# First chunk's end in another order on ScalarE and VectorE, and the upper half of the second ssm_k asked for by ScalarE

## The chip, the core and the metric

One core of one Trainium2 chip runs the whole program in one launch. The metric is the device time of an execution in microseconds; the time before is the median of three runs. Five engines work side by side, each through its own instruction stream in order: TensorE (PE), VectorE (DVE), ScalarE (ACT), GpSimd (POOL) and SyncE (SP). SyncE issues nearly all transfers; ScalarE has a queue for transfers of its own.

## The reference

Sequence length S = 2048, width D = 640, all in float32. The first block is an H3 layer with a short and a long causal convolution, the second a token-mixing MLP; both sit behind a layer norm whose scale and shift come from a conditioning vector c.

```python
mod = (_silu(c) @ w_mod).reshape(c.shape[0], 6, 1, -1)      # sa, ca, ga, sb, cb, gb
h = _layernorm(x) * (1 + ca) + sa
# _A_ref(h, k, v, ...):
k_shift = sum(k_pad[:, t:t + S, :] * shift_k[:, ks - 1 - t] for t in range(4))
kv = k_shift * v
y = irfft(rfft(kv, 2 * S) * rfft(ssm_k, 2 * S))[:S] + kv * ssm_D     # along S, per channel
x = x + ga * (h * y)
h = _layernorm(x) * (1 + cb) + sb
x = x + gb * (gelu(h^T @ w1 + b1) @ w2 + b2)^T
```

## The kernel before

The 640 channels are cut into five chunks of 128 (`c` = 0 to 4). For each chunk the long convolution is a product of transforms, made by matmuls: `step1` is the first stage of the forward transform (side 0 for kv, side 1 for ssm_k, four groups `t` each), `f2` the second stage together with the product (eight groups `g`), `i2` and `i1` the two stages back. `gate` multiplies the result by A1, the normed and scaled input, and adds it to x. After the last chunk come the second layer norm and the MLP, which fill the rest of the time with matmuls.

The order of instructions on every engine is the order in which the Python code calls them. There is no scheduler: an engine that waits at one instruction holds back all that stands behind it in its stream. The names that matter here:

- `load_ks(c)` asks for the ssm_k of a chunk, in two halves of 64 channels and 512 KB (L151), each in rows of 32 elements, and then for the two rows of ssm_D (L154), 256 bytes each. All four stand on SyncE. The data go to `KSR`, the lower columns of the tile `aux`.
- `perm_add` adds ssm_D to the first element of each channel (two operations of one partition, on VectorE for c = 1), and `perm` (L163, ScalarE) reorders the whole ssm_k into `KSP`, the tile `p`, from which `step1(1, t)` reads.
- `taps` (L169, ScalarE) spreads the four taps of the short convolution; `load_taps` fetches the next ones.
- `ac` are 16 scalings of 128 columns of x into A1 on ScalarE (L289, the first eight from tile `xa`, the others from `xb`); `po` are four multiplies and adds on VectorE, two for each half of A1, with the rows G1 and G0 that `mod_row` has made (copies on ScalarE in L360 and L362, two products on VectorE).
- `fill` is a list of the short convolution's operations for the next chunks, of which `dv(n)` puts n on VectorE. `kv_ops(2, pool)` puts one of the four groups on GpSimd.
- PSUM has three slots in rotation (`ring`). The slot of a `step1` group can be that of an `i1` half, and is then free once `gate` has read it.

The first chunk (c = 0) is special: its A1, the sums of w_mod and the mod rows all stand at its end, together with the step1 of the second chunk's kv and ssm_k. ssm_k of the second chunk goes into columns of `aux` that w_mod held, so that it can be asked for only when `mod_part` of kk = 2 has read them.

Every transfer counts on one of eight semaphores, taken in turn. A request waits for the transfer that held its semaphore last, eight requests back in the program.

Of the kernel before, what the change touches and what calls it, by code (L numbers as in the profile page):

```python
# [49 lines left out]
def mixer_kernel(ctx: ExitStack, tc: tile.TileContext, q, k, v, shift_k, ssm_k, ssm_D, w1, b1, w2, b2, c,  # L50
# [7 lines left out]
    act, dve, pool, pe, sync = nc.scalar, nc.vector, nc.gpsimd, nc.tensor, nc.sync  # L58
# [31 lines left out]
    KSR = T_aux[:, 0:2048]  # L90
# [54 lines left out]
    def load_taps(c, eng=sync):  # L145
        for h in range(2):
            eng.dma_start(TR[64 * h:64 * h + 64], dram(shift_k, (DC * c + 64 * h) * 4, [[0, 64], [1, 256]]))

    def load_ks(c, eng=sync):
        for h in range(2):  # L150
            sync.dma_start(KSR[64 * h:64 * h + 64].rearrange("p (i n) -> p i n", i=64),  # L151
                           dram(ssm_k, (DC * c + 64 * h) * S, [[32, 64], [S, 64], [1, 32]]))
        for h in range(2):
            eng.dma_start(DR[64 * h:64 * h + 1], dram(ssm_D, DC * c + 64 * h, [[64, 1], [1, 64]]))  # L154


    def perm_add(c, eng=pool):
        for h in range(2):
            r = KSR[64 * h:64 * h + 1].rearrange("p (i n) -> p i n", i=64)[:, :, 0]
            TT(eng, r, r, DR[64 * h:64 * h + 1], ALU.add)  # L160
# [6 lines left out]
    def taps():  # L167

        act.activation(TAP, TR.rearrange("p (i s) -> p s i", s=4), AF.Copy)  # L169
# [84 lines left out]
    def i2(r, eng=None):  # L254

        pp = [psum(), psum()]
        for s in range(8):
            for ri in range(2):
                for qd in range(4):
                    p = slice(32 * qd, 32 * qd + 32)  # L260
                    o, i = 512 * (qd % 2) + 64 * s, 2 * (8 * r + s)
                    pe.matmul(pp[qd // 2][:, o:o + 64], Y[p, ri, i:i + 2].rearrange("p i k -> p (i k)"),  # L262
                              V2[p, 64 * ri:64 * ri + 64], start=ri == 0, stop=ri == 1)
        for qd in range(4):
            a = 16 * (qd // 2) + 8 * r
            o = T2[:, a:a + 8, :, qd % 2]
            i = pp[qd // 2][:, 512 * (qd % 2):512 * (qd % 2) + 512].rearrange("p (a m) -> p a m", a=8)
            if eng is not None and qd > 1:
                eng.tensor_scalar(o, i, 1.0, None, op0=ALU.mult)
            else:  # L270
                act.activation(o, i, AF.Copy)  # L271
# [189 lines left out]
    def run(ops):  # L461
        for f_ in ops:
            f_()
# [47 lines left out]
    for c in range(NC):  # L511
        cn = c + 1 if c + 1 < NC else None
        ac, po = a1_ops(c)
        pend_m = pend_a = None
        for g in range(8):
            m_, a_ = f2(g)
            if pend_m:
                pend_m()
            if pend_a:
                pend_a()  # L520
            pend_a, pend_m = (pend_m and pa_next), m_
            pa_next = a_
            if c:
                for f_ in ac[2 * g:2 * g + 2]:
                    f_()
            if cn is None and g < 4:

                act.activation(X[:, 512 * g:512 * g + 1], epsc, AF.Copy)
                for b in range(2):
                    sync.dma_start(X[64 * b:64 * b + 64, 512 * g:512 * g + 512],  # L530
                                   dram(w1, (16 * b + g) * F, [[32 * F, 64], [1, 512]]))
            dv(-(-len(fill) // max((6 if c else 8) - g, 1)))
            if c and cn is not None and g == 3:
                perm_add(cn)
        pend_m()
        if pend_a:
            pend_a()
        pa_next(dve if c else pool)
        if c == 0:
            for j in range(16):  # L540
                for h in range(2):
                    dve.bn_stats(bst[:, j, h, :], XR(j, 320 * h, 320))
                dve.bn_aggr(mv[:, j, :], bst[:, j, 0:2, :])
        if c and c + 2 < NC:
            taps()
            if c + 3 < NC:
                load_taps(c + 3)
        if c == 0:
            mod_load(0, 4, P[:, 0:1920])
            for t in range(4):  # L550
                step1(0, t)
            ps = psum()
            pe.transpose(ps[:, 0:36], stg, ID[0:36, 0:36])
            act.activation(cols, ps[:, 0:36], AF.Copy)
            act.activation(sil, cols[:, 30:35], AF.Silu)
            i2(0)
            for kk in range(4):
                mod_part(tap, kk, pl[kk])
                if kk == 1:
                    sync.dma_start(T_v1[:, 0:4096], c_v1, max_dma_last_dim=4096)  # L560
                if kk == 2:
                    load_ks(1)
            rstd(rs1, nm1, 0, 16)
            run(ac[0:4])
            i2(1)
            mod_part(tap, 4, pl[4])
            load_k(2, 1)
            load_k(2, 2)
            load_v(2, 2)
            load_halo(2)  # L570
            load_k(2, 0)
            load_v(2, 0)
            load_v(2, 1)
            load_k(2, 3)
            load_v(2, 3)
            mod_sum(tap, T_kt[:, 0:640])
            run(ac[4:8])
            pool.tensor_scalar(PW, TR.rearrange("p (i s) -> p s i", s=4), 1.0, None, op0=ALU.mult)
            run(kv_ops(2, pool))
            for i in range(3):  # L580
                mod_row(i, T_kt[:, 0:640])
            taps()
            load_taps(3)
            perm_add(1, dve)
            perm(1)
            load_ks(2)
            run(ac[8:16])
            run(po[0:2])
            fill.extend(kv(3, ((0,), (1, 2), (3,))))
        elif cn is not None:  # L590
            for t in range(2):
                step1(0, t)
            perm(cn)
            if c + 2 < NC:
                fill.extend(kv(c + 3 if c + 3 < NC else None))
            else:
                fill.extend(x1s(cc, j) for cc in range(c) for j in range(16))
        else:
            blk.update({f: (j16(t[:, 0:2048]), j16(t[:, 2048:4096])) for f, t in (
                (0, mem("w0", 4096, "wb0")), (1, mem("w1", 4096, "wb1")))})  # L600
            mod_load(3, 3, T_z[:, 0:1920])
            mod_load(3, 4, P[:, 0:1920])
            for kk in range(3):
                mod_part(tap, kk, pl[kk])
            t = mem("in", 4288, "wb3")
            blk[3] = j16(t[:, 0:2048]), j16(t[:, 2048:4096])
            split_rows(0, X, (0, 1, 3))
            split_rows(1, T_aux[:, 0:2048], (0, 1, 3))
            run(po)
        if c:  # L610
            dv(7 if cn is not None else 8)
            i2(0)
            if cn is None:
                mod_part(tap, 3, pl[3])
                i2(1, dve)
                t = mem("y", 4096, "wb2")
                blk[2] = j16(t[:, 0:2048]), j16(t[:, 2048:4096])
                split_rows(0, X, (2,))
                split_rows(1, T_aux[:, 0:2048], (2,))
                break  # L620
            run(po)
            step1(0, 2)
            i2(1)
            step1(0, 3)
            dv(3)
        if c and c + 2 < NC:
            load_ks(c + 2)
        if cn == NC - 1:
            pl = [piece(T_in, 3), piece(T_in[:, 1920:3840], 3), piece(T_t, 2) + [T_rows], three(T_z),
                  three(P)]  # L630
            for kk in range(2):
                mod_load(3, kk, (T_in[:, 0:1920], T_in[:, 1920:3840])[kk])
            for j in range(3):
                sync.dma_start(pl[2][j], dram(w_mod, 256 * 6 * D + 640 * (3 + j), [[6 * D, 128], [1, 640]]))
            load_rows(1, T_aux[:, 0:2048])
        for half in range(2):
            ps = i1(half)
            if c and half:
                dv(3)
            elif c:  # L640
                k0 = step1(1, 0, True)
            elif half:
                run(po[2:4])
            gate(c, ps, half)
        spill(c)
        if c:
            k0()
        for t in range(1 if c else 0, 4):
            step1(1, t)
        if cn == NC - 1:  # L650
            dv(12)
            fill.extend(x1s(c, j) for j in range(16))
        else:
            dv(11 if c else 8)
# [397 lines left out]
    for s in range(NW):  # L1052
        i = NF + s
# [84 lines left out]
```

## Time and profile before

| | |
|---|---|
| three runs, median | 700.57 us (697.78 to 703.14) |
| profiled execution | 697.86 us |
| its span, first to last instruction | 696.1 us |
| mean granted TensorE clock | 0.975 |
| busy: PE / DVE / ACT / POOL | 89% / 71% / 42% / 18% of the span |
| the five chunks | up to about 293 us |
| HBM traffic | 72.55 MB read, 10.49 MB written |

A row of a timeline gives start and length in us, engine, line, operation, output and input, the number of merged instructions and, in brackets, the idle time ahead of it with what ended it. An `SPq` or `ACTq` row is the time that an issue takes on SyncE or ScalarE, not the transfer's. A row that begins with two times joined by a colon sums a window: its length, then the busy time and number of instructions of PE, PE's weight loads, DVE, ACT and POOL, the granted clock, the share of the transfer engines and GB/s. A row of one line's instructions gives the least, median and longest duration in ns.

### The profile page before, as it was taken

The numbers are of one execution on the slowest core, as the hardware profiler recorded it, in microseconds if no ns is written. First come the engines' busy times: TensorE is split into PE (matmuls) and PEld (weight loads), VectorE is DVE, ScalarE is ACT, GpSimd is POOL, SyncE is SP. The second block draws the span as 40 slices with busy tenths as digits, with TensorE's granted clock in tenths as the row PEclk, the third lists the DMA queues.
The fourth block names the chain that finished last, engine by engine and source line by source line (L and its number), as shares of the span: only waits on it lengthen the run. The fifth ranks groups of instructions, "written<-read, shape, count | busy, mean of one in ns | idle before, by whom it ended". The sixth has DMA issues, their size and how long they took to land.

```text
span 696.1 us, 20691 instructions
## 1 busy us (share of the span) xinstructions
PE 622.0 (89%) x9099; PEld 595.8 (86%) x9099; DVE 496.1 (71%) x866; ACT 291.6 (42%) x464; POOL 128.2 (18%) x147
## 2 busy tenths in 40 slices
PE   0689777898998988888899999999999989999997
PEld 0688466788988888778899979999999989999997
DVE  6769448978979449888985741123499868888986
ACT  0444373554746536456666232232244233233331
POOL 5184018513425025000100000000000430000000
PEclk9999798999999999999999999999999999999999
DMA  9988988627443424171305604433353533466611
GB/s 183 243 227 232 381 169 178 145 43 155 91 79 111 145 64 121 59 153 32 60 1 91 121 2 99 84 61 64 110 141 104 167 121 99 121 173 172 167 44 38
DMA packets 166930, 84.37 MB, mean 121 GB/s; under 512 B 91030, under 2 KB 157368, under 8 KB 166840
## 3 DMA queue, kind: packets, MB, share of 16 engines
q1 hardware_dynamic: 162292, 81.74, 46.9%
q10 hardware_dynamic: 4548, 1.31, 1.1%
q8 instruction: 71, 1.16, 0.7%
q14 instruction: 19, 0.16, 0.1%
HBM read 72.55 MB, written 10.49 MB: 119 GB/s over the span
## 4 chain that ended last, share of the span: by engine, by line
PE 62%; DVE 17%; DMA 6%; ACT 5%; SPq 4%; issue 3%; POOL 1%; ACTq 0%; POOLq 0%; DVEq 0%
PE pst L436 20%; PE pst L997 17%; PE pst L1074 7%; PE pst L218 5%; PE pst L233 4%; PE pst L262 4%; SPq L496 3%; DVE tap L59 3%; PE pst L282 2%; DVE p L59 2%; DMA aux<-in_A_ssm_k_dram 2%; DVE kt L59 2%; DMA w<-in_const_w_dram 1%; DMA aux<-in_w_mod_dram 1%; DVE aux L59 1%
## 5 line engine op out<-in xcount | busy, mean ns | idle before, releaser
L233 PE MATMUL pst<-z,w 128*64 128x64 f32 x2560 | 79.0, 223 | 12.0 <-ACT z L220 5.7
L233 PEld LDWEIGHTS pst<-z,w 128*64 128x64 f32 x2560 | 76.8, 138 | 14.8 <-issue 7.7
L220 ACT ACTIVATE z<-pst 128x1024 f32<-128x1024 f32 x40 | 43.0, 1076 | 51.4 <-PE pst L218 51.3
L218 PE MATMUL pst<-v,x 128*64 128x128 f32 x640 | 39.6, 282 | 27.2 <-DVE x L59 24.1
L218 PEld LDWEIGHTS pst<-v,x 128*64 128x64 f32 x640 | 36.9, 142 | 28.1 <-POOL t L459 23.6
L59 DVE TENSOR_TENSOR p<-pst,kt 128x512 f32<-128x512 f32 x80 | 50.9, 680 | 12.7 <-ACT kt L237 9.3
L59 POOL TENSOR_TENSOR y<-p 128x256 f32<-128x256 f32 x72 | 51.1, 744 | 38.8 <-DVE p L59 38.6
L218 PE MATMUL pst<-v,p 128*64 128x128 f32 x640 | 39.7, 283 | 6.8 <-DVE aux L59 4.6
L997 PE MATMUL pst<-r_z,m_w 128*128 128x320 f32 x222 | 42.1, 312 | 2.2 <-DVE m_w L59 2.2
L218 PEld LDWEIGHTS pst<-v,p 128*64 128x64 f32 x640 | 37.2, 143 | 8.0 <-DVE aux L59 4.9
L262 PEld LDWEIGHTS pst<-v,y 32*128 32x128 f32 x1280 | 39.7, 194 | 3.8 <-issue 2.6
L237 ACT ACTIVATE kt<-pst 128x512 f32<-128x512 f32 x40 | 23.9, 599 | 43.7 <-PE pst L233 30.1
L262 PE MATMUL pst<-v,y 32*128 32x64 f32 x1280 | 41.6, 279 | 0.7 <-ACT z L220 0.6
L833 ACT ACTIVATE pst<-pst,sm 128x640 f32<-128x640 f32 x13 | 10.0, 767 | 75.8 <-PE pst L436 75.8
L985 ACT ACTIVATE m_w<-m_v 128x896 fp32r<-128x896 f32 x24 | 22.7, 951 | 37.0 <-PE pst L997 16.8
L997 PEld LDWEIGHTS pst<-r_z,m_w 128*128 128x128 f32 x222 | 35.2, 190 | 2.4 <-DVE m_w L59 2.4
L59 DVE TENSOR_TENSOR tap<-tap,kt 128x512 f32<-128x512 f32 x51 | 35.5, 696 | 1.3
L59 DVE TENSOR_TENSOR kt<-in,tap 128x512 f32<-128x512 f32 x51 | 34.9, 685 | 1.4
L59 POOL TENSOR_TENSOR m_p<-u_i,r_z 128x320 f32<-128x320 f32 x1 | 0.9, 882 | 183.4 <-issue 183.4
L271 ACT ACTIVATE z<-pst 128x512 f32<-128x512 f32 x38 | 20.9, 646 | 21.9 <-PE pst L262 21.9
L59 DVE TENSOR_TENSOR m_w<-m_v,m_w 128x896 fp32r<-128x896 f32 x24 | 27.9, 1164 | 2.4 <-ACT m_w L985 1.9
L436 PE MATMUL pst<-r_z,wb0b 128*128 128x320 f32 x180 | 28.2, 310 | 0.9 <-DVE u_x L59 0.9
(289 smaller groups left out, 1445.0 us busy)
## 6 DMA issues: line engine op xcount, KB each, us to landing
x<-in_B_w_dram SPq DMA_DIRECT2D x20, 512.0 KB
aux<-in_A_ssm_k_dram SPq DMA_DIRECT2D x10, 512.0 KB
in<-in_A_k_dram SPq DMA_DIRECT2D x36, 128.0 KB
in<-in_A_v_dram SPq DMA_DIRECT2D x36, 128.0 KB
m_x<-xs SPq DMA_DIRECT2D x28, 160.0 KB
out_dram<-m_x SPq DMA_DIRECT2D x28, 160.0 KB
w<-in_const_w_dram SPq DMA_DIRECT2D x2, 2048.0 KB
m_v<-in_B_w_dram SPq DMA_DIRECT2D x9, 448.0 KB
```

Of the source, the lines that this page charges most:

```text
L59: TT = lambda eng, o, a, b, op: eng.tensor_tensor(o, a, b, op=op)
L218: pe.matmul(ps[64 * ri:64 * ri + 64, o:o + 255:2], lhs, F1[:, 128 * ri:128 * ri + 128], start=True, stop=True)
L220: evac = lambda: act.activation(Z[:, side, t], ps.rearrange("p (a k e) -> p a k e", a=4, e=2), AF.Copy)
L233: pe.matmul(ps[64 * h:64 * h + 64, o:o + 64], W2[k1 // 32][:, 2 * (k1 % 32) + ri], rhs, start=True, stop=True)
L237: act.activation(kt.rearrange("p (m i) -> p m i", i=32), pv[:, :, 1], AF.Copy)
L262: pe.matmul(pp[qd // 2][:, o:o + 64], Y[p, ri, i:i + 2].rearrange("p i k -> p (i k)"), V2[p, 64 * ri:64 * ri + 64], start=ri == 0, stop=ri ...
L271: act.activation(o, i, AF.Copy)
L436: pe.matmul(ps[0:m, h, 0:320], w_.bitcast(F32R), r_[:, 320 * h:320 * h + 320].bitcast(F32R), start=first and i == 0, stop=last and i == 2)
L496: sync.dma_start(XH[j // 8][64 * b:64 * b + 64, j % 8], dram(q, (16 * b + j) * D, [[32 * D, 64], [1, D]]))
L985: act.activation(W[n][0].bitcast(F32R), A[p, w_], AF.Copy)
L997: pe.matmul(bank[n], w[:, i].bitcast(F32R), r.bitcast(F32R), start=i == 0 and k == 0, stop=i == 6 and k == 2)
L1074: pe.matmul(acc[s][:, h, 0:320], w[:, f_].bitcast(F32R), u[r + h].bitcast(F32R), start=f_ == 0 and k == 0, stop=f_ == NF - 1 and k == 2)
```

## The change

Two things change, both at the end of the first chunk. `load_ks` gets an argument `halves`: with the lower half alone it asks for that and for ssm_D on SyncE, with the upper half alone it asks for it on ScalarE. The second call stands behind the first four scalings. And the scalings, the first half of `po` and perm change places: three scalings ahead of the mod rows instead of four, the other nine directly behind them, ahead of taps and perm; the first two operations of `po` ahead of `perm_add`.

```diff
-    def load_ks(c, eng=sync):
-        for h in range(2):
-            sync.dma_start(KSR[64 * h:64 * h + 64].rearrange("p (i n) -> p i n", i=64),
+    def load_ks(c, eng=sync, halves=(0, 1)):
+        for h in halves:
+            (act if len(halves) == 1 and h else sync).dma_start(KSR[64 * h:64 * h + 64].rearrange("p (i n) -> p i n", i=64),
                            dram(ssm_k, (DC * c + 64 * h) * S, [[32, 64], [S, 64], [1, 32]]))
-        for h in range(2):
+        for h in range(2) if 0 in halves else ():
             eng.dma_start(DR[64 * h:64 * h + 1], dram(ssm_D, DC * c + 64 * h, [[64, 1], [1, 64]]))
...
                 if kk == 2:
-                    load_ks(1)
+                    load_ks(1, halves=(0,))
             rstd(rs1, nm1, 0, 16)
             run(ac[0:4])
+            load_ks(1, halves=(1,))
             i2(1)
             mod_part(tap, 4, pl[4])
...
             mod_sum(tap, T_kt[:, 0:640])
-            run(ac[4:8])
+            run(ac[4:7])
             pool.tensor_scalar(PW, TR.rearrange("p (i s) -> p s i", s=4), 1.0, None, op0=ALU.mult)
             run(kv_ops(2, pool))
             for i in range(3):
                 mod_row(i, T_kt[:, 0:640])
+            run(ac[7:16])
             taps()
             load_taps(3)
+            run(po[0:2])
             perm_add(1, dve)
             perm(1)
             load_ks(2)
-            run(ac[8:16])
-            run(po[0:2])
             fill.extend(kv(3, ((0,), (1, 2), (3,))))
```

ScalarE at the first chunk's end, before: the scalings (L289), the eviction of i2 (L271), mod_sum (L346), the mod rows, taps, perm (L163), the last eight scalings and the first step1 of ssm_k (L220).

```order
L289 ACTIVATE aux<-xa,sm 128x128 x4
L271 ACTIVATE z<-pst_931 128x512 x2
L271 ACTIVATE z<-pst_932 128x512 x2
L346 ACTIVATE kt<-tap 96x640
L289 ACTIVATE aux<-xa,sm 128x128 x4
L360 ACTIVATE g<-pst_1039 128x640
L362 ACTIVATE g<-pst_1043 128x640
L169 ACTIVATE tap<-rows 128x256
L163 ACTIVATE p<-aux 128x32x2x32
L289 ACTIVATE aux<-xb,sm 128x128 x8
```

And the same place with the change:

```order
L289 ACTIVATE aux<-xa,sm 128x128 x4
L151 DMA aux<-in_A_ssm_k_dram 64x64x32
L271 ACTIVATE z<-pst_931 128x512 x2
L271 ACTIVATE z<-pst_932 128x512 x2
L346 ACTIVATE kt<-tap 96x640
L289 ACTIVATE aux<-xa,sm 128x128 x3
L360 ACTIVATE g<-pst_1038 128x640
L362 ACTIVATE g<-pst_1042 128x640
L289 ACTIVATE aux<-xa,sm 128x128
L289 ACTIVATE aux<-xb,sm 128x128 x8
L169 ACTIVATE tap<-rows 128x256
L163 ACTIVATE p<-aux 128x32x2x32
```

The request of the upper half stands between the first scalings and the eviction of i2, and perm is the last of the row, with no scaling behind it.

VectorE, the piece between the products on g and the conv operations (`aux<-aux,g` are the operations of `po`, `aux<-aux,rows` perm_add, `aux<-pst_1072` the gate of half 0):

```order
+L59 TENSOR_TENSOR aux<-aux,g 128x1024 x2
 L59 TENSOR_TENSOR aux<-aux,rows 1x64 x2
-L59 TENSOR_TENSOR aux<-aux,g 128x1024 x2
 L59 TENSOR_TENSOR aux<-pst_1072,aux 128x2x256x2
 L59 TENSOR_TENSOR aux<-aux,g 128x1024 x2
```

The first pair of `po` has moved ahead of perm_add; the second pair stays behind the gate of half 0.

SyncE after the constant V1 with the change, with the semaphores that a request waits for (before, a second L151 stood behind the first and took the next semaphore):

```order
L560 DMA v<-in_const_v_dram 128x4x1024 [waits DMAHW5_49,DMAHW6_49,DMAHW2_49,PE_49]
L151 DMA aux<-in_A_ssm_k_dram 64x64x32 [waits DMAHW7_49,DMAHW4_49,PE_49]
L154 DMA rows<-in_A_ssm_D_dram 1x64 x2
L131 DMA in<-in_A_k_dram 64x8x64
L131 DMA in<-in_A_k_dram 64x8x64 [waits DMAHW0_49]
L131 DMA in<-in_A_k_dram 64x8x64 [waits DMAHW1_49]
L131 DMA in<-in_A_k_dram 64x8x64 [waits DMAHW2_49]
L137 DMA in<-in_A_v_dram 64x8x64 [waits DMAHW3_49]
L137 DMA in<-in_A_v_dram 64x8x64 [waits DMAHW4_49]
```

ssm_D and the k loads of the next chunk have moved up to the lower half. Semaphore 3 is that of the upper half on ScalarE, semaphore 4 that of the lower half, so that the first v request still waits for a half of ssm_k (before, the lower half held 3 and the upper 4).

## The prediction

> **What bounds the kernel now.** I read the chain of waits first, since the change touches one stage of some 40 us in a span of 696.1 us and only the chain says whether that stage is on the path. Its answer around the end of the first chunk, in order of time (start, length, what):
>
> ```profile
> 81.22 0.64 SPq L151
> 81.91 15.10 DMA aux<-in_A_ssm_k_dram
> 97.59 1.81 issue
> 99.41 3.19 ACT aux L289 x8
> 102.62 2.22 DVE aux L59
> 104.86 2.18 DVE aux L59
> 107.14 1.24 DVE aux L59
> 108.42 5.90 PE pst L218 x64
> 114.34 1.07 ACT z L220
> 115.45 2.11 PE pst L233 x64
> 117.59 0.61 ACT kt L237
> 118.22 1.29 DVE p L59 x2
> ```
>
> So the path is: ssm_k asked for at 81.22 and landed at about 97.0; then not the reordering of ssm_k (perm) itself, but what stands behind it on ScalarE, the last eight scalings of A1 (L289); then two multiplies of A1 on VectorE (4.4 us), the gate (1.24), two of the four matmul groups of step1, f2 and the first product at 118.22. The timelines of ScalarE, VectorE and TensorE show why the eight scalings are late:
>
> ```profile
> 83.12 1.65 ACT L289 ACTIVATE aux<-xa,sm 128x128 f32<-128x128 f32 x4 [6.73 <-PE tap L342]
> 87.40 2.17 ACT L271 ACTIVATE z<-pst 128x512 f32<-128x512 f32 x4 [2.63 <-PE pst L262]
> 89.99 1.65 ACT L289 ACTIVATE aux<-xa,sm 128x128 f32<-128x128 f32 x4
> 91.56 0.70 ACT L360 ACTIVATE g<-pst 128x640 f32<-128x640 f32 x1
> 92.75 0.66 ACT L169 ACTIVATE tap<-rows 128x256 f32<-128x256 f32 x1
> 97.38 2.16 ACT L163 ACTIVATE p<-aux 128x2048 f32<-128x2048 f32 x1 [3.97 <-DVE aux L59]
> 99.41 3.18 ACT L289 ACTIVATE aux<-xb,sm 128x128 f32<-128x128 f32 x8
> 92.30 1.55 DVE L59 TENSOR_TENSOR g<-pst,g 128x640 f32<-128x640 f32 x2 [14.37 <-ACT g L360]
> 97.03 0.26 DVE L59 TENSOR_TENSOR aux<-aux,rows 1x64 f32<-1x64 f32 x1 [0.78 <-DMA aux<-in_A_ssm_k_dram]
> 97.33 2.48 DVE L59 TENSOR_TENSOR aux<-aux,g 128x1024 f32<-128x1024 f32 x2
> 102.62 4.41 DVE L59 TENSOR_TENSOR aux<-aux,g 128x1024 f32<-128x1024 f32 x2 [1.47 <-ACT aux L289]
> 99.59 4.17 PE L218 MATMUL pst<-v,p 128*64 128x128 f32 x64 [1.09 <-ACT p L163]
> 108.42 5.87 PE L218 MATMUL pst<-v,p 128*64 128x128 f32 x64 [4.65 <-DVE aux L59]
> ```
>
> ScalarE stands idle 3.97 us at perm, and VectorE does only two small adds (perm_add) between 93.85 and 97.33, while work that needs neither ssm_k waits behind them in program order. Then TensorE idles 4.65 us with half of step1 done.
>
> Whether time won here lasts is read from VectorE in the f2 loop that follows:
>
> ```profile
> 108.28 0.69 DVE L59 TENSOR_TENSOR tap<-in,tap 128x512 f32<-128x512 f32 x1
> 118.22 1.29 DVE L59 TENSOR_TENSOR p<-pst,kt 128x512 f32<-128x512 f32 x2 [1.98 <-ACT kt L237]
> 118.20:136.10 17.90, 14.71 (x456) 14.27 (x454) 17.61 (x29) 10.59 (x24) 10.15 (x17) 1.00 0.69 160
> ```
>
> In the window (third number group: VectorE) it works 17.61 of 17.90 us: there is no slack in which a gain could vanish, and the chain from 134 to 373 us holds TensorE, VectorE and ScalarE work, no transfer. So the first product's start, 118.22, is the measure: what it moves by, the end moves by.
>
> **The change, part by part.**
>
> *Order on ScalarE and VectorE.* Nothing is added there but one DMA issue. One scaling leaves the first group: 3 of 4 at 0.41 from 89.99 end at 91.2. The two copies of L360/L362 then start at 91.15 and end at 92.4, and nine scalings follow at 3.18/8 = 0.40 each: done at 96.0. taps (L169, 0.66) ends at 96.6, and perm may start there at the earliest. VectorE: its two products on g start 0.4 earlier, 91.9 to 93.45; the first pair on A1 2.48, to 95.95; then the two perm_adds at 0.26. All of this now runs in the time in which both engines waited. If ssm_k came at 93 instead of 97, that cover would be gone and the moved pieces would bind: perm at 96.6, not at 93.3.
>
> *Landing of ssm_k.* The requests and the transfer:
>
> ```profile
> 72.00:88.00 16.00, 11.56 (x189) 6.27 (x190) 5.20 (x18) 5.98 (x12) 1.37 (x2) 0.79 1.03 400
> 92.00:97.00 5.00, 4.27 (x167) 4.13 (x171) 1.81 (x3) 1.41 (x3) 0.00 (x0) 0.66 0.77 126
> 81.22 10.74 SPq L151 DMA_DIRECT2D aux<-in_A_ssm_k_dram  x2
> L151 SPq DMA_DIRECT2D aux<-in_A_ssm_k_dram x10: 595/1138/10046, 11.5 to 188.3; - x10
> 92.01 2.63 SPq L154 DMA_DIRECT2D rows<-in_A_ssm_D_dram  x2
> 13.43 1.15 ACTq L147 DMA_DIRECT2D rows<-in_A_shift_k_dram  x2
> 11.47 4.93 SPq L151 DMA_DIRECT2D aux<-in_A_ssm_k_dram  x2
> ```
>
> Up to 88 the engines move w_mod and the constant V1 at 400 GB/s; after 92 it is 126 GB/s, ssm_k in its short rows. The first half's request takes 0.64 us; the second held SyncE for 10.05, and ssm_D another 2.3: a request waits until the half before it has passed. In the change the upper half goes out on ScalarE at 83.12 + 1.65 = 84.8, behind four scalings. The bytes are the same and so are the 16 engines, so the earliest bound is what a shared rate gives. Two halves of 0.52 MB at 126 GB/s are 8.3 us from about 88: 96.3. The late bound is today's 97.0, plus nothing if the two merely alternate. The upper half may also slip in among V1's rows before 88, or ssm_D and the lower half may come last; I take perm_add at 97.0, perm at 97.35 as now, and keep 96.6 for perm as the good end.
>
> The Trainium skill, "DMA: Bandwidth & Descriptors", section "Rules for kernel authors", speaks against this part: transfers from two issuing engines interleave on the same 16 engines, so two halves gain no bandwidth and only the issue time is saved. By it perm stays at 97.35, the value I take anyway; no run here has shown two queues on such halves yet.
>
> *The issue on ScalarE.* The nearest rows: first halves take 0.6 us (the least of ten L151 issues is 0.595). ScalarE is idle 2.63 us before 87.40, so 0.6 is covered and costs nothing; beyond 2 us the cover is gone, and the eviction of i2(1), mod_sum, the scalings, taps and perm are queued behind it. The other end is 10.05. I take 0.6: this ring holds nothing else then, and while SyncE hung in L151 from 11.47 to 16.4, ScalarE issued two requests of 0.57 each at 13.43.
>
> *After perm.* perm ends at 99.5. VectorE: gate 0 from 97.3 to 98.6 (1.24); the second pair on A1, its scalings long done, 2.48 if GpSimd is still idle, 4.41 if it runs: 101.1 to 103.0; gate 1 to 102.4 to 104.3. TensorE: four groups of step1 with no hole, 4 x 2.08 = 8.3, to 107.9 (the third needs the PSUM slot that gate 1 frees by 104.3; it would start at 103.7). The second pair now costs 5.87 against 4.17 for the first; its window carries a lower clock:
>
> ```profile
> 106.00:112.00 6.00, 3.58 (x34) 3.58 (x36) 5.72 (x8) 0.00 (x0) 5.73 (x4) 0.50 0.80 174
> ```
>
> Granted clock 0.50. The Trainium skill, "TensorE: Matmul & The Clock Gate", Part 1, says that a TensorE left idle for a window of some 3.4 us falls to half rate. By that the lost clock goes with the hole; if it stayed, TensorE's path below would be 1.7 us later.
>
> Eviction 1.1, f2 2.14, copy 0.6: TensorE's path allows the first product at 111.8 (111.0 with the early perm). VectorE's path: eleven conv operations, 108.28 to 116.24 now, 7.97 us, from gate 1: 110.4 to 112.3.
>
> *The third limit: k of the chunk after.* Those conv operations read k(2,0), which SyncE asks for behind ssm_k:
>
> ```profile
> 94.69 3.10 SPq L131 DMA_DIRECT2D in<-in_A_k_dram  x4
> 100.77 1.28 SPq L131 DMA_DIRECT2D in<-in_A_k_dram  x2
> 101.24 2.51 POOL L59 TENSOR_TENSOR t<-in,t 128x512 f32<-128x512 f32 x2 [23.31 <-DMA in<-in_A_k_dram]
> 109.48 3.23 SPq L151 DMA_DIRECT2D aux<-in_A_ssm_k_dram  x2
> ```
>
> The first four requests end at 97.79 and GpSimd starts on their data at 101.24, 3.45 later; so k(2,0), asked for by 102.05, is there at about 105.5 today, unseen behind 108.28. In the change SyncE is rid of one long wait, but ssm_D still queues behind the lower half, and the first v request waits for the slot of the upper half, which now lands no sooner than 96 to 97. The requests for k(2,0) so end between 100.8 and 102.8. The data are there at 104.2 to 106.2; I take 105.0. VectorE then stands idle from 102.4 or so, and the first product comes at 105.0 + 7.97 = 113.0. That is the latest of the three limits (111.8, 112.3, 113.0): what is late next is a load. What else hangs on the moved steps has room: the taps and the ssm_k of the chunk after are asked for at 108 to 109.48, after taps and perm in both orders, and GpSimd, whose sums follow the products, is busy 10.15 of the 17.90 us above.
>
> *Sum.* 118.22 - 113.0 = 5.2 us off the profiled time of 697.86 (span 696.1): 692.7. The median of the three runs shown is 700.57, 2.7 above the profiled run, so the forecast on that scale is **695.4 us**, 0.7% less. Its own bounds: perm early and k early give 7.2, k late gives 4.0.
>
> **The rivals.**
>
> *All three limits give way at once* (faster by more). The upper half moves among V1's rows, SyncE is free earlier, k(2,0) lands by 103, perm starts at 96.6: the first product at 111.0, 7.2 us won, 693.4. For it: 10.05 us of SyncE's time go free. Against: 126 GB/s is the transfer, not the request.
>
> *The wait changes its place.* ScalarE's ring is served only when SyncE's runs empty, that is when SyncE stops at the v request: the upper half lands at about 101. perm then ends at 103.5, TensorE's path gives 115.8, and k(2,0), asked for by 105.2, lands at 108.7, plus 7.97: 116.6. Gain 1.6, 699.0. Against it: at 13.43 ScalarE's requests went out while SyncE's stood still.
>
> *ScalarE is held in the request* (the other side). Place: L151 on ScalarE at 84.8. Price: all that ScalarE does up to perm is late by the hold less the 2.0 us of cover. TensorE's path of 111.8 has 0.75 us of slack at perm (96.6 against 97.35), so it gives 111.8 + hold - 2.75. From a hold of 9.2 us on the kernel is slower. With SyncE's 10.05 that is 0.9 us lost, 701.5; if it also stands through the second half as ssm_D did (10.05 + 2.33), 3.2 us, 703.8. For it: the ten requests of L151 reach 10.05. Against: that one stood behind a half on its own ring.
>
> **How the numbers follow.** Forecast 58%, all three limits giving way 20%, the wait moved 12%, ScalarE held 10%. Faster or slower by 1%, 7 us, is about what a measurement of this kernel can tell from no change. Over 1% faster takes most of the second case (0.14) and the quarter of the first that the spread of three runs (697.78 to 703.14) carries over it (0.15): 0.29. Over 1% slower: part of the held case, and what an unseen collision behind it would add: 0.11. Within 1%: 0.60. The range reaches from 691.0 (the good case with the runs' spread below it) to 700.5 (the moved wait with it above); it leaves out the held case and the far tail.
>
> **What would show each step.** Right: L163 on ScalarE at 97 to 98 with nine scalings ahead of it, directly followed by L220; the second pair on A1 near 2.5 us; TensorE's L218 as one run of 128 in about 8.3 us; VectorE idle 1 to 3 us on a k load before its conv operations; the first product at 113; L151 on ScalarE at 0.6. Wrong: L151 on ScalarE over 2 us; perm after 99; a first product that is 5 us earlier while the end is not, which would mean slack between 136 and 373 us that I did not see.

## The result, and the profile after

The changed kernel takes 692.58 us in the median of six runs (690.7 to 695.51), the kernel before 700.46 in six runs beside them (697.78 to 704.97): a ratio of 0.989, 95% interval 0.984 to 0.993. In a later measurement it was 693.95 (eight runs) against 699.1 (31 runs), ratio 0.993 (0.990 to 0.996). So the change makes the kernel faster by 5 to 8 us, 0.7 to 1.1%; the forecast was 5.2 us less and 695.4 us. The profiled execution took 692.01 us with a span of 690.1 (before 697.86 and 696.1).

One thing about times is needed first. The program up to this place does not take the same time in every execution. I take as entry the start of the fourth part of mod_part, the second L342 that reads w_mod from aux, before and in the changed kernel:

```profile
82.36 1.28 PE L342 MATMUL tap<-aux,sm 128*32 128x320 f32 x12 [1.19 <-DMA aux<-in_w_mod_dram]
```

```profile
83.28 1.28 PE L342 MATMUL tap<-aux,sm 128*32 128x320 f32 x12 [1.20 <-DMA aux<-in_w_mod_dram]
```

That difference of 0.92 arises ahead of anything the change touches. Times below are of the traces; "on before's line" means with what entry is later than 82.36 taken off (0.92 here), "from entry" means after that start.

ScalarE after, the rows that answer to those of the prediction (start, length, engine, line, operation, count, idle time ahead):

```profile
85.08 0.63 ACTq L151 DMA_DIRECT2D aux<-in_A_ssm_k_dram  x1
88.33 2.17 ACT L271 ACTIVATE z<-pst 128x512 f32<-128x512 f32 x4 [2.63 <-PE pst L262]
94.06 3.19 ACT L289 ACTIVATE aux<-xb,sm 128x128 f32<-128x128 f32 x8
97.14 0.65 ACT L169 ACTIVATE tap<-rows 128x256 f32<-128x256 f32 x1
97.91 2.18 ACT L163 ACTIVATE p<-aux 128x2048 f32<-128x2048 f32 x1
112.08 0.60 ACT L237 ACTIVATE kt<-pst 128x512 f32<-128x512 f32 x1 [2.18 <-PE pst L233]
```

The request takes 0.63 us, and the eviction of i2 (L271) still has its 2.63 us of idle time ahead: it is covered. The scalings and taps run on into perm with no hole where 3.97 us of idle time stood before.

VectorE and GpSimd:

```profile
94.87 2.48 DVE L59 TENSOR_TENSOR aux<-aux,g 128x1024 f32<-128x1024 f32 x2
97.27 0.56 DVE L59 TENSOR_TENSOR aux<-aux,rows 1x64 f32<-1x64 f32 x2
99.00 3.43 DVE L59 TENSOR_TENSOR aux<-aux,g 128x1024 f32<-128x1024 f32 x2
102.53 1.23 DVE L59 TENSOR_TENSOR aux<-pst,aux 128x1024 f32<-128x1024 f32 x1
103.68 0.68 DVE L59 TENSOR_TENSOR tap<-in,tap 128x512 f32<-128x512 f32 x1
110.94 0.70 DVE L59 TENSOR_TENSOR tap<-tap,kt 128x512 f32<-128x512 f32 x1
112.71 1.29 DVE L59 TENSOR_TENSOR p<-pst,kt 128x512 f32<-128x512 f32 x2 [1.08 <-ACT kt L237]
99.61 3.96 POOL L59 TENSOR_TENSOR t<-in,t 128x512 f32<-128x512 f32 x2 [21.20 <-DMA in<-in_A_k_dram]
```

No wait for ssm_k is left ahead of perm_add (97.27), and none for k ahead of the conv operations (103.68). The conv operations end at 111.64 and VectorE then waits 1.08 us for the copy (L237): in this execution TensorE's path sets the first product.

TensorE and a window that answers to the one of granted clock 0.50:

```profile
100.15 1.09 PE L218 MATMUL pst<-v,p 128*64 128x128 f32 x14 [0.92 <-ACT p L163]
102.32 6.49 PE L218 MATMUL pst<-v,p 128*64 128x128 f32 x114 [1.09 <-issue]
109.95 4.41 PE L233 MATMUL pst<-z,w 128*64 128x64 f32 x142 [1.14 <-ACT z L220]
128.96 3.71 PE L218 MATMUL pst<-v,x 128*64 128x128 f32 x64 [0.44 <-DVE p L59]
```

```profile
107.00:113.00 6.00, 4.86 (x137) 4.62 (x134) 4.71 (x8) 2.75 (x3) 5.77 (x5) 1.00 0.90 174
112.70:130.60 17.90, 15.03 (x456) 14.45 (x454) 17.61 (x29) 10.62 (x24) 13.72 (x18) 1.00 0.81 172
```

The 4.65 us hole between the two halves of step1 is gone, and so is the half clock behind it (1.00 now). All four groups take 100.15 to 108.81, 8.66 us, of which 1.09 is a hole for which the trace names no wait. VectorE does the f2 loop in the same 17.61 of 17.90 us. The first product moved from 118.22 to 112.71, the next step1 of kv behind the loop from 134.46 to 128.96, and the first matmuls after the norm of the second block as the ends of the two chains show, first before, then after:

```profile
373.49 26.52 PE pst L436 x179
```

```profile
367.55 28.43 PE pst L436 x192
```

The gain of 5.5 us (6.4 from entry) is still there 250 us later, 5.9; nothing between swallows it. SyncE after:

```profile
82.13 0.64 SPq L151 DMA_DIRECT2D aux<-in_A_ssm_k_dram  x1
82.83 9.81 SPq L154 DMA_DIRECT2D rows<-in_A_ssm_D_dram  x2
92.68 4.23 SPq L131 DMA_DIRECT2D in<-in_A_k_dram  x4
99.30 1.88 SPq L131 DMA_DIRECT2D in<-in_A_k_dram  x2
```

The hold (the time for which a request keeps its engine) did not go: ssm_D now stands 9.81 us behind the lower half, as the upper half did before (10.05). But with one hold instead of two, the k requests start 9.40 us from entry instead of 12.33.

### The profile page after: what moved, and what is told of

It reads as the page before. It is cut to its first block, busy times and chain, and to the rows that moved or that the text cites. A ratio compares the mean times of both kernels' runs of the same rounds, so it can differ in the third digit from the quotient of the medians.

```text
span 690.1 us, 20692 instructions
## 1 busy us (share of the span) xinstructions
PE 619.0 (90%) x9099; PEld 592.5 (86%) x9099; DVE 495.3 (72%) x866; ACT 291.8 (42%) x464; POOL 127.9 (19%) x147
## 3 DMA queue, kind: packets, MB, share of 16 engines
q8 instruction: 71, 1.16, 0.7%
## 4 chain that ended last, share of the span: by engine, by line
PE 62%; DVE 16%; SPq 7%; DMA 5%; ACT 4%; issue 3%; POOL 2%; ACTq 0%; POOLq 0%; DVEq 0%
PE pst L436 20%; PE pst L998 17%; PE pst L1075 7%; PE pst L218 5%; PE pst L262 4%; PE pst L233 4%; SPq L496 3%; DVE tap L59 3%; DVE kt L59 2%; PE pst L282 2%; DMA in<-in_A_k_dram 2%; DVE p L59 2%; SPq L131 1%; SPq L154 1%; DMA aux<-in_w_mod_dram 1%
## 5 line engine op out<-in xcount | busy, mean ns | idle before, releaser
L220 ACT ACTIVATE z<-pst 128x1024 f32<-128x1024 f32 x40 | 43.0, 1074 | 47.2 <-PE pst L218 47.0
L237 ACT ACTIVATE kt<-pst 128x512 f32<-128x512 f32 x40 | 23.9, 597 | 42.5 <-PE pst L233 24.9
L218 PE MATMUL pst<-v,p 128*64 128x128 f32 x640 | 37.6, 274 | 3.0 <-issue 2.1
L218 PEld LDWEIGHTS pst<-v,p 128*64 128x64 f32 x640 | 35.2, 137 | 4.2 <-issue 2.7
L271 ACT ACTIVATE z<-pst 128x512 f32<-128x512 f32 x38 | 20.8, 640 | 21.5 <-PE pst L262 21.5
```

The costliest lines, as they stand in the source:

```text
L218: pe.matmul(ps[64 * ri:64 * ri + 64, o:o + 255:2], lhs, F1[:, 128 * ri:128 * ri + 128], start=True, stop=True)
L220: evac = lambda: act.activation(Z[:, side, t], ps.rearrange("p (a k e) -> p a k e", a=4, e=2), AF.Copy)
L237: act.activation(kt.rearrange("p (m i) -> p m i", i=32), pv[:, :, 1], AF.Copy)
```

## The experiments

Theory A: the gain is the order, and the request on ScalarE brings ssm_k in no sooner. Theory B: two queues bring ssm_k, or the k loads behind it, in sooner, and the request has a share of its own.

**The order alone**, both halves on SyncE:

```diff
-                    load_ks(1, halves=(0,))
+                    load_ks(1)
             rstd(rs1, nm1, 0, 16)
             run(ac[0:4])
-            load_ks(1, halves=(1,))
```

> Both halves of the second ssm_k on SyncE as before; only the order on ScalarE and VectorE is the change's. All times on the time line of before (third mod_part at 79.89). Theory A (the prediction's: order alone wins, the request on ScalarE buys no landing time): ssm_k lands at 97.0, perm at 97.4, first product at 112 to 113, as with the whole change; 5 to 6 us won. Theory B (two queues move the short rows faster, so the request has a share of its own): perm again at 97.4, but k(2,0) is asked for as late as before, by 102.05, and binds VectorE: conv operations from 104.3 to 105.5, first product at 112.3 to 113.5, 0.5 to 1.5 us behind the whole change.

Measured 695.87 us, ratio 0.995 (0.992 to 0.998). VectorE:

```profile
97.31 0.62 DVE L59 TENSOR_TENSOR aux<-aux,rows 1x64 f32<-1x64 f32 x2
99.10 2.47 DVE L59 TENSOR_TENSOR aux<-aux,g 128x1024 f32<-128x1024 f32 x2
105.72 0.70 DVE L59 TENSOR_TENSOR tap<-in,tap 128x512 f32<-128x512 f32 x1 [2.81 <-DMA in<-in_A_k_dram]
113.59 1.28 DVE L59 TENSOR_TENSOR p<-pst,kt 128x512 f32<-128x512 f32 x2
```

Entry is 82.49 here. The product comes 31.10 us from entry, 4.8 sooner than before (35.86), 1.7 later than in the whole change (29.43). VectorE stands 2.81 us on k(2,0): the third limit of the prediction, which the whole change does not show, binds here. perm_add did not wait for ssm_k in this execution, though it is on one queue. So theory A is right on ssm_k, and theory B on k: conv operations at 105.6 on before's line (B said 104.3 to 105.5), and a product 1.7 us behind the whole change (B said 0.5 to 1.5).

**The request alone**, in the old order:

```diff
-            run(ac[4:7])
+            run(ac[4:8])
...
-            run(ac[7:16])
...
-            run(po[0:2])
             perm_add(1, dve)
             perm(1)
             load_ks(2)
+            run(ac[8:16])
+            run(po[0:2])
```

> The upper half asked for by ScalarE, the order of before. Here VectorE has nothing between its products on g and perm_add, so the second perm_add starts when ssm_k has landed. Theory A: it starts at 96.3 to 97.0, nothing else moves, first product at 118, time as before within 1 us. Theory B (163 GB/s against 126 in the five microseconds around the landing): it starts at 93.9 to 95.5, perm ends by 97.5, the eight scalings by 100.5, gate 1 by 105.5, first product at 113 to 114.5: 3.5 to 5 us won by the request alone, so that the two parts of the change would stand in for each other.

Measured 699.4, ratio 1.001 (0.998 to 1.004): worth nothing. The timelines of VectorE and ScalarE, entry 82.78:

```profile
96.71 0.55 DVE L59 TENSOR_TENSOR aux<-aux,rows 1x64 f32<-1x64 f32 x2 [2.43 <-DMA aux<-in_A_ssm_k_dram]
97.34 2.20 ACT L163 ACTIVATE p<-aux 128x2048 f32<-128x2048 f32 x1 [3.51 <-DVE aux L59]
99.43 3.17 ACT L289 ACTIVATE aux<-xb,sm 128x128 f32<-128x128 f32 x8
102.63 4.32 DVE L59 TENSOR_TENSOR aux<-aux,g 128x1024 f32<-128x1024 f32 x2 [1.52 <-ACT aux L289]
118.61 1.29 DVE L59 TENSOR_TENSOR p<-pst,kt 128x512 f32<-128x512 f32 x2 [2.46 <-ACT kt L237]
```

From entry the second perm_add starts some 0.5 us sooner than before (the merged row holds both adds; before, the second began at 97.03), and the eight scalings behind perm set the end as they did. The landing that theory B named here, 93.9 to 95.5 on before's line, did not come: the half microsecond is all there is, and it lies within what one queue alone varies (the order alone with k(2,0) first, below, has its second perm_add 15.6 us from entry, before 14.7). For ssm_k itself B falls.

**The whole change again**, beside these two:

> The whole change once more, for a comparison on the same chip. First product 6.4 us earlier than before, counted from the third mod_part; 692 us, ratio 0.989 to 0.992. Both theories alike.

693.95, ratio 0.993 (0.990 to 0.996), product 29.12 us from entry. It is 1.9 us below the order alone, as the traces' 1.7 to 2.0 say, though the intervals overlap: the size of the request's share rests on the traces. All of them agree: in the five with the new order and two queues the product comes 28.8 to 29.4 us from entry, in the two with the new order and one queue at 31.1 and 31.2.

What the second queue does shows in the traffic. The same window in four kernels, 6 to 12 us from entry; the last number is GB/s, the one before it the share of the transfer engines. Before, order alone, request alone, whole change:

```profile
88.36:94.36 6.00, 3.63 (x91) 2.80 (x92) 1.55 (x2) 5.05 (x11) 0.00 (x0) 0.84 1.12 163
```

```profile
88.49:94.49 6.00, 3.65 (x59) 2.31 (x60) 1.23 (x2) 4.87 (x12) 0.00 (x0) 0.68 1.16 131
```

```profile
88.78:94.78 6.00, 3.57 (x104) 2.78 (x105) 1.55 (x2) 5.05 (x11) 0.00 (x0) 0.88 1.31 212
```

```profile
89.28:95.28 6.00, 3.62 (x99) 2.79 (x100) 1.97 (x3) 5.70 (x14) 0.00 (x0) 0.85 1.25 208
```

With two queues it is 208 to 212 GB/s here, with one 131 to 163. The same window is at 200 to 224 in three of the other traces with the new order and two queues, but at 154 in that of the last experiment below, so the rate is not a sure sign. In steps of 1.5 us most of the difference lies 9.0 to 10.5 us from entry: 50 and 57 GB/s with one queue, 209 and 216 with two. Whether that is the upper half of ssm_k or k is open, as the windows do not split the bytes by tensor. What does agree in all is the requests: with two queues SyncE begins to ask for k 2.6 to 2.9 us sooner than before in the two kernels shown, and is done with k(2,0) 17.2 to 18.3 us from entry, against 19.7 before and 20.6 with the order alone (where the requests stand in the same order). The prediction weighed a rule of the Trainium skill, "DMA: Bandwidth & Descriptors", "Rules for kernel authors": a second issuing engine saves issue time only. For ssm_k the runs agree: no landing sooner by more than half a microsecond. But the issue time saved is no small thing here, since a request behind a half is held for 10 us.

**k(2,0) ahead of v**, to see whether the third limit is the request or the transfer; once on the order alone, once on the whole change:

```diff
-            load_v(2, 2)
             load_halo(2)
             load_k(2, 0)
+            load_v(2, 2)
```

> The order alone (both halves on SyncE), with the request for v(2,2) moved behind those for the halo and k(2,0), so that k(2,0) is asked for 1.3 to 2.4 us earlier. Theory B (in the order alone VectorE's conv operations wait 2.81 us for k(2,0), and this wait is what the request on ScalarE buys off): conv operations start 1.3 to 2.4 us earlier than in the order alone, product at 111.5 to 112 on before's time line, as in the whole change. Other theory (the load is bound by transfer rate, not by its request): conv start and product within 0.5 us of the order alone.

> The whole change with the same move of v(2,2). Theory B: conv operations start when gate 1 ends, with no wait; the product is then bound by TensorE's path, 0 to 0.5 us gained on the change, not to be seen in the time.

These two and the last two below were measured beside another 31 runs of before, median 700.49. On the order alone 695.5, ratio 0.994 (0.991 to 0.996), as without it (0.995). Entry 83.82:

```profile
99.45 0.26 DVE L59 TENSOR_TENSOR aux<-aux,rows 1x64 f32<-1x64 f32 x1 [1.24 <-DMA aux<-in_A_ssm_k_dram]
107.15 0.70 DVE L59 TENSOR_TENSOR tap<-in,tap 128x512 f32<-128x512 f32 x1 [2.47 <-DMA in<-in_A_k_dram]
```

The request ended 1.9 us sooner from entry (18.71 against 20.63), the data came no sooner: the conv operations start at 23.33 against 23.23. So the transfer sets when k is there, not the request, on the one queue. One thing weakens this: in this execution ssm_k itself came later, and perm_add waited 1.24 us for it, so all transfers may have been late by up to 1 us; the request was early by nearly twice that. On the whole change 693.16, ratio 0.990 (0.987 to 0.993), the same as the change within the intervals, product 29.29 us from entry against 29.12 and 29.43. The conv operations start there with gate 1's end and no wait for k, as expected; but gate 1 came late, since the second pair on A1 took 4.34 us beside GpSimd, and the product follows the conv operations and not TensorE's path.

**perm in two halves**, on the whole change, to see what TensorE's path is worth when step1 may start on half of perm:

```diff
-    def perm(c):
+    def perm(c, parts=1):
+        for p_ in range(parts):     # i-range 32*p_//parts to 32*(p_+1)//parts
...
-            perm(1)
+            perm(1, 2)
```

> The change, with perm in two operations of half the size, so that step1 of ssm_k can start on the first. Both theories: TensorE's path binds the first product in the changed kernel, with step1 waiting 0.92 us for perm; the two halves take 1.1 to 1.3 us each, step1 starts 0.9 us earlier, the first product 0.8 to 0.9 earlier, VectorE's conv operations (7.97 from gate 1) then bind. 0.5 to 0.9 us off the changed kernel, seen in the profile and not in the ratio.

696.07, ratio 0.994 (0.991 to 0.997): no gain, if anything 2 us lost against the change (intervals overlap). Its profiled execution, 689.98, is 6 us below its own median, so the trace is read for positions only. TensorE, GpSimd and VectorE (the step1 line is L220 in this kernel, two lines further down):

```profile
100.19 1.09 PE L220 MATMUL pst<-v,p 128*64 128x128 f32 x14
105.16 3.71 PE L220 MATMUL pst<-v,p 128*64 128x128 f32 x64 [0.57 <-DVE aux L59]
99.09 3.51 POOL L59 TENSOR_TENSOR t<-in,t 128x512 f32<-128x512 f32 x2 [22.04 <-DMA in<-in_A_k_dram]
99.51 4.17 DVE L59 TENSOR_TENSOR aux<-aux,g 128x1024 f32<-128x1024 f32 x2
```

step1 starts with no wait for perm, and its second half then waits for gate 1, whose second pair on A1 took 4.17 us beside GpSimd. Product 29.39 us from entry: what TensorE wins, VectorE holds back.

**Both halves asked for by ScalarE**, the other-side rival made real:

```diff
-            (act if len(halves) == 1 and h else sync).dma_start(
+            (act if len(halves) == 1 else sync).dma_start(
...
-                    load_ks(1, halves=(0,))
...
+            load_ks(1, halves=(0,))
             load_ks(1, halves=(1,))
```

> The change, with both halves of the second ssm_k asked for by ScalarE behind the first four scalings, and ssm_D on SyncE as before. On before's time line. Prediction's rival (a request is held while a half ahead of it on its own ring has not passed): the first request 0.6 us, the second held for 5 to 7 us, to about 91 or 92; the eviction of i2 starts 4 to 5 us late, perm at 101 to 102, the first product at 115.5 to 117, 1 to 2.5 us won on before and 4 to 5 lost on the change. Other theory (the hold belonged to SyncE's ring, full of V1 and w_mod): the second request 0.6 us too, perm at 97, product as in the change. By both, SyncE's k requests start at once, at 84 to 88.

705.97, ratio 1.008 (1.005 to 1.011): slower. Entry 83.27, as in the whole change. ScalarE, then VectorE and TensorE:

```profile
85.73 8.49 ACTq L151 DMA_DIRECT2D aux<-in_A_ssm_k_dram  x1
94.26 2.12 ACT L271 ACTIVATE z<-pst 128x512 f32<-128x512 f32 x4 [8.58 <-issue]
108.14 2.11 ACT L163 ACTIVATE p<-aux 128x2048 f32<-128x2048 f32 x1 [3.33 <-POOL t L59]
101.92 3.54 DVE L59 TENSOR_TENSOR aux<-aux,g 128x1024 f32<-128x1024 f32 x2
105.38 2.68 DVE L59 TENSOR_TENSOR aux<-aux,rows 1x64 f32<-1x64 f32 x2
97.00 2.53 PE L353 MATMUL pst<-kt,sm 1*128 1x320 f32 x12 [7.52 <-ACT kt L346]
110.30 9.98 PE L218 MATMUL pst<-v,p 128*64 128x128 f32 x128 [3.37 <-ACT p L163]
```

And a window of it at the start of step1:

```profile
110.00:114.00 4.00, 3.70 (x36) 3.70 (x38) 3.86 (x3) 0.25 (x1) 2.65 (x1) 0.50 0.75 130
```

The second request is held 8.49 us, behind the first on the same queue. L271 is 5.9 us late against the change (94.26 against 88.33): the hold less the idle time of 2.63. Then it grows: the mod row's matmuls (L353) take 2.53 instead of 1.37 after 7.52 us of idle time, at a granted clock of 0.50; VectorE's pair takes 3.54 instead of 2.48 and the two adds of one partition 2.68 instead of 0.56 beside GpSimd, and perm is 10.2 us late, which is these four together (5.9, 1.2, 1.1, 2.1). Its step1 starts at the clock of 0.50 again and is 9.98 us long instead of 8.66. The product comes 40.9 us from entry, 5.0 later than before; the medians say 5.5. The expectation had put it 1 to 2.5 us ahead of before: it had put the hold at 5 to 7 us and left out what follows it. The release that the profile names for perm is GpSimd's operation that ends at 107.93; the adds end at 108.06, and perm starts at 108.14.

**The first chunk's ssm_k on two queues as well**:

```diff
-    load_ks(0, act)
+    load_ks(0, act, halves=(0,))
+    load_ks(0, act, halves=(1,))
```

> The whole change, and the upper half of the first ssm_k, at the program's start, asked for by ScalarE too. There ScalarE waits for this landing (21.00 us in before) and nothing on the path does, so it measures the landing alone. Theory of two rings (212 to 224 GB/s against 132 to 163 in the six microseconds of short rows): landing by 18 to 19.5. Theory of one shared rate: 20.5 to 21.2. Time as the change's within 1 us by both.

694.71, ratio 0.992 (0.990 to 0.995), as the change without it. perm_add, which stands on GpSimd in this chunk:

```profile
21.85 0.35 POOL L59 TENSOR_TENSOR aux<-aux,rows 1x64 f32<-1x64 f32 x1 [2.62 <-issue]
```

SyncE comes to the v loads at 12.54, 4 us sooner than before (16.52), but the add on the second half, for which GpSimd stands idle 2.62 us, starts at 21.85, against 21.07 before and 22.10 in the change. The earlier landing that the faster-queue theory asked for failed a second time: the transfer engines then move 204 GB/s between 11 and 22 us, before 193 and the change 183, so what they move more is probably not ssm_k but the loads that go out sooner.

## Why the prediction was right, and where it was off

**What bounded the kernel** was read rightly: undoing the order (the request alone) brings the old time back, 699.4 against 699.1, and the order alone gives most of the gain.

**ssm_k no earlier.** Forecast perm_add at 97.0 and perm at 97.35; on before's line the adds began at 96.35 and perm at 96.99. The prediction's reason was the landing of ssm_k; in the trace perm_add does not wait for it. perm starts 0.08 us after perm_add's end and 0.12 after the taps', and in the second execution (entry 83.50) it is VectorE's add for which it stands idle:

```profile
98.20 2.20 ACT L163 ACTIVATE p<-aux 128x2048 f32<-128x2048 f32 x1 [0.23 <-DVE aux L59]
```

So what sets perm is the work moved ahead of it, first VectorE's (the products on g, the pair on A1, the two adds), with ScalarE's scalings and taps done just before. The prediction named that as what would bind if ssm_k came early, and took 96.6 for it. The two limits lie close: with the request alone, where nothing stands ahead of perm_add, ssm_k let the adds begin at 96.3 on before's line. perm's place was right within 0.4 us, its reason was not.

**The request on ScalarE** 0.6 forecast, 0.63 measured, with the cover untouched. With both halves on that queue it is held 8.49 us: the place and the mechanism of the other-side rival are shown, and that it is the half ahead on the same queue that holds. Its price was set too low. By the prediction's formula a hold of 8.49 gives a product at 117.5 on before's line; it came at 123.3. Missing were the longer times of the mod row's matmuls and of step1 at a clock of 0.50 (1.2 and 1.3 us) and of VectorE beside GpSimd (3.2).

**After perm.** The second pair was put at 2.48 to 4.41, and took 3.43 and 2.47 in two executions; step1 was put at 8.3 in one run, and took 8.66 with a hole of 1.09; the clock went back to 1.00 with the hole. The first product by TensorE's path was put at 111.8; on before's line it is 111.79. That it fits to 0.01 is luck: the 0.36 us won at perm and the 0.36 lost in step1 cancel. And step1's 8.3 was itself too long, since it doubled the first half's 4.17: in one run without a hole it took 7.21 and 7.68 (k(2,0) first on the order alone, the first chunk's ssm_k too).

**The step that was mis-sized is the third limit.** It put k(2,0) at 105.0 (104.2 to 106.2), the product at 113.0 and the gain at 5.2. The chain of waits after has the load (start, length):

```profile
99.95 3.39 DMA in<-in_A_k_dram
```

It lands by 103.34, 102.4 on before's line, 1.8 sooner than the low bound. Two terms were too long: the requests end at 100.26 on before's line, not 100.8 to 102.8, and the data come 2.2 us behind, not 3.45. The k load was therefore hidden behind gate 1, by some 0.3 us, the limit was TensorE's path, and the gain 6.4 us from entry. In the second execution VectorE did idle ahead of the conv operations:

```profile
104.63 0.69 DVE L59 TENSOR_TENSOR tap<-in,tap 128x512 f32<-128x512 f32 x1 [1.54 <-ACT z L220]
```

The profile names ScalarE's L220, but in the first execution the conv operations start before that L220 ends, so k(2,0) is the likelier cause. On before's line that is 103.5, again sooner than the low bound of 104.2; the conv operations end at 112.60 and TensorE's copy at 112.59, so the two limits meet, and the product comes 29.12 us from entry. With the order alone the third limit is there at nearly the forecast size: conv operations at 105.6 on before's line and the product at 113.5. The prediction had in effect worked out that kernel, and given k next to nothing for the request on ScalarE: 105.0 instead of the 105.5 of before.

**The wait that moves** to another place, the rival priced at 699.0, did not show: by it perm would end at 103.5, and it ended at 99.2 on before's line. **All limits giving way**, 7.2 us, needed k by 103 and perm at 96.6: the first came, the second nearly, and step1's hole kept the rest.

**No slack in the f2 loop**: shown, by 17.61 of 17.90 us in both kernels and by the 5.5 to 5.9 us that last to 367 us. The end itself is less exact: from the first product to the end the ten traces take 575.3 to 580.3 us with no relation to what was changed. That, and the up to 2 us ahead of entry, is as large as the difference between the two measurements of the change, 7.9 and 5.2 us.

What stays open is where that variation comes from, and the "issue" holes of up to 2.1 us on TensorE that change their places between executions.

## What to carry to other kernels

When an engine waits for a transfer, look first at what stands behind the waiting instruction and does not need the transfer: moving it ahead was worth 4.8 us at the first product here and 3.2 us in the medians, while moving half of the transfer to a second queue was worth nothing alone, and some 2 us on top of the new order, through the loads queued behind it. The next limit is then a load whose landing the old order hid, and it has to be sized from its own requests in the new order, not from the old ones. A request on a second queue is cheap (0.63 us) as long as it is the first of its kind there; the next one behind it held its engine for 8.49 us.

## What the runs showed of the hardware that was not expected

- The hold belongs to what is ahead on the queue, not to the size of the request: ssm_D, two rows of 256 bytes, held SyncE 9.81 us behind a half of ssm_k. Where both halves stand on ScalarE, the same two requests took 0.65 us on SyncE, right behind V1 with its 2 MB. So not every transfer ahead holds; a half, 512 KB in rows of 128 bytes, does.
- The times of VectorE's operations with two inputs go with when GpSimd starts. The second pair on A1 takes 2.47 us where GpSimd starts 1.5 us or more behind it (four kernels, among them the whole change again and the order alone), 3.43 where GpSimd starts at 99.61, 0.61 behind it, and 4.17 to 4.51 where GpSimd starts ahead of it (five kernels). The Trainium skill, "SBUF — State Buffer", section "SBUF: two separate sides", says that the two engines lock a shared port for a whole instruction and the loser waits; the adds of one partition, 0.26 us each alone, that took 2.68 for two beside GpSimd fit that. No run here took GpSimd away to test it.
- The granted clock was 0.50 behind the holes of 4.65 us and, in an experiment, of 7.52 us, and 1.00 where the hole of 4.65 us was gone, as the Trainium skill, "TensorE: Matmul & The Clock Gate", Part 1, has it. But it is not only such long holes: around the mod row the clock is 0.50 for some microseconds in the kernel before too (92.86 to 94.36), where from 83.56 on no hole of TensorE is longer than 1.61 us, and in the order alone the mod row's matmuls took 2.23 us at a clock of 0.58, behind a hole of 1.62. So the 1.16 us that they lost behind the hole of 7.52 can't be put down to that hole alone.
